# A fused banded attention and two-layer block on one core: the planner of all engines' orders gets other durations, a model of transfers, and a pass back and forth

## The chip, the cores and the metric

The kernel runs on one core of a Trainium2 chip. The metric is the device time of one execution in microseconds (us). Three runs of the kernel before took 677.65, 678.53 and 680.7 us, a median of 678.53 us.

## The reference

Attention over 4 batches, 8 heads, 768 positions, 64 wide, keeps for each query the first 4 keys (sinks) and the last 128 keys. Its output, 3072 tokens of 512, goes through two matrix products with a gate between them.

```python
scores = scale * np.matmul(q, k.transpose(0, 1, 3, 2))
keep = is_sink | in_window              # key < 4, or 0 <= query - key < 128
a = softmax(np.where(keep, scores, -1e9))
x = np.matmul(a, v)                     # then (3072, 512)
h = x @ w_in                            # (512, 2048)
g = h - np.tanh(h)
return g @ w_out                        # (2048, 512)
```

## The kernel before

**Tiles.** The 3072 tokens are 12 chunks of 256. A chunk's attention is four units, one for each pair of heads. The 2048 hidden columns are 8 groups of 256. One step is one chunk with one group; 96 steps, listed in `order`, are the two-layer block. Each step has a first half (24 matmuls at L807 into a double-buffered PSUM tile `h`), a gate, and a second half (L877, or from chunk 5 on L911, which computes 2x2 blocks of the product with seven products instead of eight). All products are split into a high and a low part. In the seven-product form the gate is a chain: tanh on ACT (L826), a difference (L829) and three sums (L840 to L842) on DVE, a copy to the high part on ACT (L845), and the low part on DVE (L848). One buffer, `gbuf`, is held from its tanh to its low part.

**A unit of attention** loads keys and queries (L347, and L356 or L104), computes scores on PE (L517 for the first 12 units, L524 later), masks and reduces them on DVE (`merge`: L539 and L541), takes exp and scales on ACT (L549, L575), turns them on PE (L609), masks them (L616 to L629), and multiplies by the values on PE (L666, L672). The result becomes `xall` on ACT and DVE (L688, L692).

**Weights** arrive as 64-bit words (`wraw`, L402), are decoded on DVE (L156 to L160) and split. The first matrix is written back to memory (`wscr`) and, from chunk 3 on, streamed through a ring of seven slots (`ring` and `spare`, L792); four slots make one step's weights. Sums of blocks of the second matrix are made by a copy and an accumulating transfer (`derive`, L1006 and L1009).

**Queues.** SP issues the loads of the first 12 units, weights, ring and most stores; GpSimd (POOL) issues keys, queries and values of later units, the accumulating transfers and most stores of the result. An engine executes in the order in which its instructions were emitted, so one that waits holds all behind it on that engine.

**The order is planned.** Nothing is emitted while the program is described: each piece of work is put into `Work` with its engine, a duration, a due time, and the names it reads and writes. `Work.order` then simulates all engines. At each moment it takes, of the pieces that are ready, the one with the smallest due time. The pieces are emitted by their simulated start, and that is each engine's order on the chip; the simulated times themselves do not reach the chip. Due times come from formulas with constants (`due_step`, `due_unit`, `due_group`). In the planner before, a transfer keeps SP occupied for `lands` ns and its data is there 1700 ns later, or 4372 ns (`LAND`) later for pieces due after 65222 (`LATE`); from then on the durations of ACT, DVE and POOL are also multiplied by 1.05. Pieces marked `port` wait while one marked so runs on the other of DVE and POOL.

The lines that the steps below speak of:

```python
n = min((n for n in waiting[e] if at(n, e) <= t), key=lambda n: (self.all[n][2], n))   # due time decides
...
todo, _ = work.order()
for n in todo:
    work.all[n][3]()                    # emitted in the order of simulated starts
```

Of the kernel before, what the change touches and what calls it, by code (L numbers as in the profile page):

```python
# [32 lines left out]
NG = 8  # L33
# [135 lines left out]
class Work:  # L169
# [3 lines left out]


    WAKE = {"PE": 250, "ACT": 170, "DVE": 90, "POOL": 100, "SP": 80}

    def __init__(self, slack, pad, late, land):
        self.all, self.wrote, self.read = [], {}, {}
        self.slack, self.pad, self.late, self.land = slack, pad, late, land

    def add(self, engine, took, due, fn, reads=(), writes=(), lands=0, port=False):
# [10 lines left out]
        self.all.append((engine, took, due, fn, after - {n}, lands, port))  # L192

    def order(self):
        todo = {}
        for n, (engine, *_) in enumerate(self.all):
            todo.setdefault(engine, []).append(n)
        users, left = [[] for _ in self.all], [len(t[4]) for t in self.all]
# [3 lines left out]
        ready = {n: 0.0 for n, k in enumerate(left) if k == 0}  # L202
        waiting = {e: [n for n in v if n in ready] for e, v in todo.items()}
        free, port, start, done = dict.fromkeys(todo, 0.0), {}, {}, {}

        def at(n, e):
            t = max(free[e], ready[n])
            return max(t, port.get("DVE" if e == "POOL" else "POOL", 0.0)) if self.all[n][6] else t

        while any(waiting.values()):  # L210
            t, e = min((min(at(n, e) for n in v), e) for e, v in waiting.items() if v)
            n = min((n for n in waiting[e] if at(n, e) <= t), key=lambda n: (self.all[n][2], n))
            _, took, _, _, _, lands, locks = self.all[n]
            took *= self.pad if e in ("ACT", "DVE", "POOL") and self.all[n][2] > self.late else 1.0
            waiting[e].remove(n)
            start[n], free[e], done[n] = t, t + took, t + took
            if lands:
                free[e], done[n] = t + (took if e == "POOL" else lands), t + lands + (1700 if self.all[n][2] < self.late else self.land)
            if locks:
                port[e] = t + took  # L220
            for u in users[n]:
                f = self.all[u][0]
                lag = 0 if f == e else self.WAKE[e]
                if f == "PE":
                    lag += self.slack if self.all[u][2] > self.late else 100
                ready[u] = max(ready.get(u, 0.0), done[n] + lag)
                left[u] -= 1
                if not left[u]:
                    waiting[f].append(u)
# [3 lines left out]
def _banded(tc, qd, kp, vp, vs, masks, w_in, w_out, ident, pts, early, out):  # L233
    nc = tc.nc
    et = mybir.EngineType
    with ExitStack() as ctx:
# [27 lines left out]
        RAW, TWO, CUT, DUO, SC, PB, ZL, TK = 12, 12, 2, 3, 4, 4, -4000, 1100  # L264
        SLK, PAD, LATE, LAND, QP, KP, BP, LEAD3 = 0.0, 1.05, 65222.0, 4372.0, 0, 0, 1, 89032.0
        SA, NSLOT, RING, GP, LQ, ST = 5, 7, 7, 0, 1, 1
        work = Work(SLK, PAD, LATE, LAND)
# [61 lines left out]
        def load_qk(u):  # L329
# [36 lines left out]
            if raw(u):  # L366
                work.add("POOL", 460, t - ZL, zeros, (), [slots(u)[1]])
# [6 lines left out]
        def load_v(cc):  # L374
# [19 lines left out]
            work.add("POOL" if LQ and cc > 3 else "SP", 500 * took, due_unit(4 * cc), values, (), [vslot[cc, i] for i in new] + ["seq v"],  # L394
                     lands=1000 * took)

        def load_w(k, g):
# [10 lines left out]
            for z in range(2):  # L408
                work.add("SP", 500, t, lambda z=z: words(z), (), [("wr", k, g, z)] + old, lands=2050)
# [28 lines left out]
        work.add("POOL", 900, 1500, sink_start, (), ["sidei", "vsink"] + [("z", i) for i in range(NPAIR)])  # L438
        work.add("ACT", 600, 0, rest, (), ["mask"])
        count = [0]  # L440

        def sink_values(b, due):
# [23 lines left out]
            work.add("SP", 400, due - 9000, load, (), [slot], lands=300)  # L466
            work.add("ACT", 500, due - 3500, high, [slot], ["vsink"])
            work.add("POOL", 1000, due - 3000, low, ["half", "vsink"], [slot], port=True)
            work.add("DVE", 500, due - 1000, total, [slot], ["vsink"], port=True)
# [4 lines left out]
        def split(u):  # L474
# [26 lines left out]
            work.add("ACT", 525, t, q_high, q, ["qh"] + old)  # L501
            work.add("POOL" if QP else "DVE", 1360 if QP else 705, t, q_low, q + ["qh"], ["ql"], port=True)
            for h in range(2):
                work.add("ACT", 425, t, lambda h=h: k_high(h), k, [("ks", h)] + old)
                work.add("POOL" if KP else "DVE", 1050 if KP else 590, t, lambda h=h: k_low(h), k, [("ks", h)], port=True)

        def scores(u, t):
# [48 lines left out]
            if raw(u):  # L556
                src, took = slots(u), 890
# [805 lines left out]
```

## Time and profile before

| | us |
|---|---|
| median of three runs | 678.53 (677.65 to 680.7) |
| span of the profiled execution, first to last instruction | 676.2 |
| PE busy | 655.5 (97%) |
| PE weight loads busy | 603.3 (89%) |
| DVE busy | 531.8 (79%) |
| ACT busy | 412.6 (61%) |
| POOL busy | 204.0 (30%) |

The page gives the profiled execution by its span; a whole-execution time of that same run is not listed, and the median of the runs is 2.3 us above the span. Transfers took 153 MB, 226 GB/s over the span: 57.4% of the 16 DMA engines' time went to the queue that SP fills (q1), 16.4% to the one that POOL fills (q0). The mean granted TensorE clock was 0.997 of full speed. The page's slices show PE at 60% in the first fortieth, 80% in the second, at 90% or more in 37 more, and at 50% in the last.

### The profile page before, as it was taken

The page shows a single profiled execution, that of the slowest core. Times are in us where ns is not written, and L with a number is a line of the kernel's source. Part 1 is how long each engine was busy: PE and PEld are TensorE (multiplying, and loading weights), DVE is VectorE, ACT ScalarE, POOL GpSimd, SP SyncE. Part 2 cuts the span into 40 slices and gives each one's busy share as a digit, 9 for nine tenths or more (in the row PEclk, how much of TensorE's full clock was granted, in tenths as well). Part 3 has the DMA queues.
Part 4 walks back from the last instruction along what each step waited for, and adds up shares of the span by engine and source line. Part 5 has one row for each costly group of instructions (what it writes and reads, how often), then busy time and mean ns, then how long its engine had stood idle before and what let it go on. Part 6 is the DMA issues. An engine that isn't in the chain of part 4 may idle for free.

```text
span 676.2 us, 14570 instructions
## 1 busy us (share of the span) xinstructions
PE 655.5 (97%) x5099; PEld 603.3 (89%) x5099; DVE 531.8 (79%) x1365; ACT 412.6 (61%) x1056; POOL 204.0 (30%) x363
## 2 busy tenths in 40 slices
PE   6899999999999999999999999999999999999995
PEld 4677899998988899889999999999999999999995
DVE  6889998964898975567798898888988878855654
ACT  4986443435998876556776667567667567632331
POOL 5454000001995443344523323332223322300100
PEclk9999999999999999999999999999999999999998
DMA  5878797786998677799977767867777766657861
GB/s 177 266 262 269 266 295 263 270 287 175 191 203 274 203 217 223 227 280 266 300 217 240 224 199 207 260 196 203 227 231 216 242 199 199 198 165 207 270 198 37
DMA packets 79341, 152.96 MB, mean 226 GB/s; under 512 B 9564, under 2 KB 25564, under 8 KB 79260
## 3 DMA queue, kind: packets, MB, share of 16 engines
q1 hardware_dynamic: 65884, 121.65, 57.4%
q0 software_dynamic: 13376, 30.30, 16.4%
q8 instruction: 42, 0.69, 0.4%
q14 instruction: 39, 0.32, 0.1%
HBM read 131.47 MB, written 20.45 MB: 225 GB/s over the span
## 4 chain that ended last, share of the span: by engine, by line
PE 73%; ACT 7%; DVE 5%; DMA 5%; POOL 4%; issue 4%; POOLq 0%; SPq 0%; DVEq 0%; ACTq 0%
PE h L807 30%; PE s L911 10%; PE o L911 7%; PE o L877 6%; PE x L672 3%; PE s L877 3%; DMA w<-bscr 2%; PE t L609 2%; PE t L672 2%; PE t L877 2%; PE t L524 2%; PE x L877 2%; ACT p L575 2%; PE x L524 1%; ACT p L549 1%
## 5 line engine op out<-in xcount | busy, mean ns | idle before, releaser
L807 PE MATMUL h<-xall,ring 128*128 128x256 f32 x990 | 130.9, 279 | 0.0
L807 PEld LDWEIGHTS h<-xall,ring 128*128 128x128 f32 x990 | 121.2, 188 | 0.9 <-PE t L672 0.2
L826 ACT ACTIVATE gbuf<-h 128x512 f32<-128x512 f32 x96 | 57.1, 595 | 84.6 <-PE h L807 55.2
L356 POOL DMA_DIRECT2D qraw<-qd x36 | 29.3, 813 | 222.4 <-DVE q L496 198.0
L807 PE MATMUL h<-xall,spare 128*128 128x256 f32 x738 | 96.2, 277 | 0.0
L807 PEld LDWEIGHTS h<-xall,spare 128*128 128x128 f32 x738 | 90.0, 188 | 0.5
L549 ACT ACTIVATE p<-p,st 128x132 f32<-128x132 f32 x168 | 66.9, 400 | 26.8 <-DVE st L541 25.5
L845 ACT CAST ghbuf<-gbuf 128x896 fp32r<-128x896 f32 x55 | 51.9, 943 | 49.3 <-DVE gbuf L842 48.8
L848 DVE TENSOR_TENSOR glbuf<-gbuf,ghbuf 128x896 fp32r<-128x896 f32 x55 | 60.3, 1096 | 19.7 <-ACT ghbuf L845 16.0
L575 ACT ACTIVATE p<-p,st 128x132 f32<-128x132 f32 x168 | 54.2, 394 | 3.9 <-DVE st L570 3.5
L829 DVE TENSOR_TENSOR gbuf<-h,gbuf 128x512 f32<-128x512 f32 x55 | 37.8, 687 | 19.1 <-ACT gbuf L826 18.7
L877 PE MATMUL o<-w,ghbuf 128*128 128x512 f32 x192 | 50.8, 399 | 0.3
L629 POOL TENSOR_TENSOR pt<-pt,after 128x512 f32<-128x512 f32 x32 | 44.4, 1386 | 22.0 <-ACT pt L626 21.3
L807 PE MATMUL h<-xall,w 128*128 128x256 f32 x384 | 50.5, 282 | 0.0
L807 PEld LDWEIGHTS h<-xall,w 128*128 128x128 f32 x384 | 48.5, 188 | 1.6
L829 DVE TENSOR_TENSOR h<-h,gbuf 128x512 f32<-128x512 f32 x41 | 28.5, 694 | 19.1 <-ACT gbuf L826 19.0
L488 DVE TENSOR_TENSOR ks<-kraw,ks 64x392 fp32r<-64x392 f32 x72 | 40.4, 562 | 3.4 <-ACT ks L483 1.1
L877 PEld LDWEIGHTS o<-w,ghbuf 128*128 128x128 f32 x192 | 33.8, 188 | 6.8 <-ACT ghbuf L832 0.9
L623 DVE TENSOR_TENSOR pt<-t,below 128x512 f32<-128x512 f32 (+1 forms) x48 | 28.8, 600 | 12.6 <-PE t L609 7.4
L483 ACT CAST ks<-kraw 64x392 fp32r<-64x392 f32 x72 | 37.1, 515 | 2.2 <-DMA kraw<-kp 1.4
L911 PE MATMUL s<-edge,ghbuf 128*128 128x256 f32 x220 | 35.5, 280 | 0.1
L835 DVE TENSOR_TENSOR glbuf<-h,ghbuf 128x512 fp32r<-128x512 f32 x41 | 28.1, 685 | 9.1 <-ACT ghbuf L832 9.1
(174 smaller groups left out, 1560.8 us busy)
## 6 DMA issues: line engine op xcount, KB each, us to landing
ring<-wscr SPq DMA_DIRECT2D x165, 256.0 KB, 4.3
spare<-wscr SPq DMA_DIRECT2D x123, 256.0 KB, 4.6
qraw<-qd POOLq DMA_DIRECT2D x36, 256.0 KB, 5.0
wraw<-w_in SPq DMA_DIRECT2D x16, 512.0 KB, 6.0
wraw<-w_out SPq DMA_DIRECT2D x16, 512.0 KB, 5.7
wscr<-w SPq DMA_DIRECT2D x16, 512.0 KB, 6.0
kraw<-kp POOLq DMA_DIRECT2D x36, 196.0 KB, 4.6
v<-vp POOLq DMA_DIRECT2D x18, 256.0 KB, 3.4
```

Source lines behind the costliest of these rows:

```text
L483: nc.scalar.copy(ks[u][r, h, :], kt[u][r, :])
L488: (nc.gpsimd if KP else nc.vector).tensor_tensor(k[o, h, :], t[r, :], k[r, h, :].bitcast(F32), op=ALU.subtract)
L549: nc.scalar.activation(e, e, AF.Exp, bias=st[u][:, j : j + 1], scale=-1.0, accum_out=st[u][:, 4 + j : 5 + j],)
L575: nc.scalar.activation(pr[u][:, j, :], pr[u][:, j, :], AF.Copy, scale=s[:, 8 + j : 9 + j])
L629: nc.gpsimd.tensor_tensor(w[:, :, 0, :], w[:, :, 0, :], after.unsqueeze(1).to_broadcast([P, 4, P]), op=ALU.mult)
L807: nc.tensor.matmul(hps[n][:, f, :], lhsT=w, rhs=x, start=r == 0, stop=r == 11)
L826: nc.scalar.activation(g0, h(), AF.Tanh)
L829: nc.vector.tensor_tensor(g0 if strassen(n) else h(), h(), g0, op=ALU.subtract)
L845: nc.scalar.copy(ghbuf[:, n % 2], gbuf[:, 1:, :])
L848: nc.vector.tensor_tensor(glbuf[:, :7, :], gbuf[:, 1:, :], ghbuf[:, n % 2].bitcast(F32), op=ALU.subtract)
L877: nc.tensor.matmul(sums_of(n, cc, t), lhsT=a[:, f, t * P : (t + 1) * P], rhs=wt[1, g][:, (0, 1, 0)[i], f, :], start=first and not low and ...
L911: nc.tensor.matmul(acc, lhsT=a[:, b, :], rhs=factor(g, m, part % 2), start=g == 0 and part == 0 and m in (4, 1, 2, 7), stop=closes(n) and ...
```

## The change

`Work` is replaced and the figures handed to it are changed; what is computed, the tiles, and the due-time formulas stay.

1. Durations and wake-up times between engines are other numbers (DVE pieces of 705 become about 605; a masked `merge` goes from 880 to 1091; a first-half piece on PE from 722 to 685). The 1.05 factor and the constants `SLK`, `PAD`, `LATE`, `LAND`, `TK` go. Every result that goes from another engine to PE counts as 400 ns later (`SLACK`).
2. All transfers share one "mover": each carries `moves`, the time it takes there, and has landed `LOAD` = 2700 (or `STORE` = 1400) after its turn. SP is occupied only for the issue and issues at most 1000 ns (`AHEAD`) before the mover is free.
3. `order` first packs with the due times, then packs backward from the end with the reversed order as rank, then forward again with the backward pass's start times as rank (`TURNS` = 1). That last pass gives the order.
4. The tokens "seq k" and "seq q", which kept the loads of keys and those of queries in order among themselves, go; "seq v" stays.
5. `x_high` makes its tiles at its first call in whatever order, where it did so in the call for the first pair.

```diff
-    WAKE = {"PE": 250, "ACT": 170, "DVE": 90, "POOL": 100, "SP": 80}
+    WAKE = {"PE": 200, "ACT": 150, "DVE": 118, "POOL": 75, "SP": 80}
+    AHEAD, SLACK = 1000, 400
...
+    def lag(self, a, u):
+        e, lands = self.all[a][0], self.all[a][5]
+        return (lands or (0 if e == self.all[u][0] else self.WAKE[e])) + self.SLACK * (e != "PE" and self.all[u][0] == "PE")
+
+    def pack(self, rank, back=False):
+
+        users = [[] for _ in self.all]
         for n, t in enumerate(self.all):
             for a in t[4]:
                 users[a].append(n)
+        then = [t[4] for t in self.all] if back else users
+        left = [len(u) if back else len(t[4]) for u, t in zip(users, self.all)]
+        ready, waiting, free, start = {}, {t[0]: [] for t in self.all}, {}, {}
...
         def at(n, e):
+            t, moves = ready[n], self.all[n][7]
+            if back and moves:
+                t = max(t, free.get("mover", 0.0)) + moves
+            elif moves and e == "SP":
+                t = max(t, free.get("mover", 0.0) - self.AHEAD)
+            t = max(t, free.get(e, 0.0))
+            return max(t, free.get("port of DVE" if e == "POOL" else "port of POOL", 0.0)) if self.all[n][6] else t
 
         while any(waiting.values()):
             t, e = min((min(at(n, e) for n in v), e) for e, v in waiting.items() if v)
-            n = min((n for n in waiting[e] if at(n, e) <= t), key=lambda n: (self.all[n][2], n))
-            _, took, _, _, _, lands, locks = self.all[n]
-            took *= self.pad if e in ("ACT", "DVE", "POOL") and self.all[n][2] > self.late else 1.0
+            n = min((n for n in waiting[e] if at(n, e) <= t), key=lambda n: (rank[n], -n if back else n))
             waiting[e].remove(n)
-            start[n], free[e], done[n] = t, t + took, t + took
-            if lands:
-                free[e], done[n] = t + (took if e == "POOL" else lands), t + lands + (1700 if self.all[n][2] < self.late else self.land)
...
+            _, took, _, _, _, _, port, moves = self.all[n]
+            start[n] = t
+            free[e] = done = t + took
+            if port:
+                free["port of " + e] = done
+            if moves:
+                free["mover"] = t if back else max(done, free.get("mover", 0.0)) + moves
+                done = done if back else free["mover"]
+            for u in then[n]:
+                lag = self.lag(u, n) if back else self.lag(n, u)
+                ready[u] = max(ready.get(u, 0.0), done + lag)
                 left[u] -= 1
                 if not left[u]:
-                    waiting[f].append(u)
+                    waiting[self.all[u][0]].append(u)
+        return start
+
+    def order(self):
+        start = self.pack([t[2] for t in self.all])
+        for _ in range(self.turns):
+            last = self.pack({n: -s - self.all[n][1] for n, s in start.items()}, back=True)
+            start = self.pack({n: -s - self.all[n][1] for n, s in last.items()})
         return sorted(start, key=lambda n: (start[n], n)), start
...
-            work.add(e, 600, t, keys, (), [slots(u)[0], "seq k"], lands=800 if raw(u) else 1000)
-            work.add(e, 800, t, queries, (), [slots(u)[1], "seq q"], lands=600 if raw(u) else 1000)
+            work.add(e, 430 if raw(u) else 564, t, keys, (), [slots(u)[0]], lands=LOAD, moves=630)
+            work.add(e, 1120 if raw(u) else 745, t, queries, (), [slots(u)[1]], lands=LOAD, moves=424 if raw(u) else 848)
...
-            work.add("DVE", 880 if kind else 450, d + 1000, merge, s + ["mask"] * (0 < kind), [("p", slot(u), i) for i in range(t, 2)])
+            work.add("DVE", 1091 if kind else 434, d + 1000, merge, s + ["mask"] * (0 < kind), [("p", slot(u), i) for i in range(t, 2)])
...
-            work.add("SP", 400, d, copied, src, w + old, lands=took + 100)
-            work.add("POOL", 650, d, added, src, w, lands=1000 + 600 * n)
+            work.add("SP", 430, d, copied, src, w + old, lands=LOAD, moves=424 * n)
+            work.add("POOL", 585, d, added, src, w, lands=LOAD, moves=809 * n)
...
-                    work.add("SP", 500, due_step(n) - STREAM + 700 * j, lambda j=j: stream(n, j),
-                             [("scr", g, j // 2)], [("ring", ring_at(n, j))] + ([("w", 0, 1)] if cc == 3 and g == 0 else []), lands=850)
+                    work.add("SP", 320, due_step(n) - STREAM + 700 * j, lambda j=j: stream(n, j),
+                             [("scr", g, j // 2)], [("ring", ring_at(n, j))] + ([("w", 0, 1)] if cc == 3 and g == 0 else []), lands=LOAD, moves=810)
...
-                    work.add("PE", 722, due_step(n) - LAST * (n == NS - 1), some, x + [w], [("h", n % 2)])
+                    work.add("PE", 685, due_step(n) - LAST * (n == NS - 1), some, x + [w], [("h", n % 2)])
```

## Rows read from the trace of the kernel before

**Rows 1.** The page's first part: busy us, share of the span and instructions by engine.
```profile
PE 655.5 (97%) x5099; PEld 603.3 (89%) x5099; DVE 531.8 (79%) x1365; ACT 412.6 (61%) x1056; POOL 204.0 (30%) x363
```
**Rows 2.** Busy time by stretch; its first line names the columns.
```profile
core 0: us, PE busy (x) PEld busy (x) DVE busy (x) ACT busy (x) POOL busy (x), PEclk, DMA share, GB/s
0.00:20.00 20.00, 13.05 (x53) 9.38 (x54) 12.58 (x71) 11.16 (x42) 10.37 (x36) 1.00 0.59 182
20.00:75.00 55.00, 51.12 (x342) 40.10 (x341) 50.50 (x158) 42.97 (x146) 21.75 (x44) 1.00 0.80 264
...
150.00:225.00 75.00, 73.38 (x503) 64.53 (x502) 60.73 (x181) 60.53 (x175) 46.77 (x70) 1.00 0.85 218
...
350.00:600.00 250.00, 248.94 (x2201) 240.87 (x2200) 213.41 (x571) 163.26 (x406) 73.05 (x128) 1.00 0.70 214
...
650.00:676.20 26.20, 19.21 (x155) 17.98 (x153) 13.04 (x24) 5.81 (x8) 0.00 (x0) 0.92 0.31 94
```
**Rows 3.** PE's waits over the span: total us, times, longest.
```profile
PE s L517 <- DMA qk<-qd: 3.3, 2, 1.7
...
PE t L609 <- ACT pt L616: 1.9, 3, 1.0
```
**Rows 4.** SP's timeline from 6.5 to 17 us: start, duration, line, transfer.
```profile
8.39 1.05 SPq L391 DMA_DIRECT2D v<-vp  x2
9.49 0.43 SPq L347 DMA_DIRECT2D qk<-kp  x1
...
11.17 0.67 SPq L446 DMA_DIRECT2D vraw<-vs  x1
11.89 0.43 SPq L402 DMA_DIRECT2D wraw<-w_in  x1
12.36 0.43 SPq L347 DMA_DIRECT2D qk<-kp  x1
```
**Rows 5.** DVE's waits from 12 to 20 us.
```profile
DVE st L569 <- ACT wide L549: 1.2, 1, 1.2
DVE wide L541 <- PE s L517: 1.1, 1, 1.1
```
**Rows 6.** DVE's timeline: one masked merge, its first instruction and the next piece's.
```profile
17.93 0.27 DVE L539 COPY_PREDICATED o<-above,o 128x128 f32<-128x128 uint32 x1
...
19.01 0.73 DVE L461 SCALAR_TENSOR_TENSOR vsink<-vsink,sides,vraw 64x128 fp32r<-64x128 f32 x2
```
**Rows 7.** SP's timeline from 57 to 75 us.
```profile
58.11 6.33 SPq L391 DMA_DIRECT2D v<-vp  x3
64.49 0.90 SPq L402 DMA_DIRECT2D wraw<-w_in  x2
```
**Rows 8.** The timeline near the end: one gate's first and last instruction.
```profile
658.71 0.60 ACT L826 ACTIVATE gbuf<-h 128x512 f32<-128x512 f32 x1 [1.68 <-PE h L807]
...
662.17 1.09 DVE L848 TENSOR_TENSOR glbuf<-gbuf,ghbuf 128x896 fp32r<-128x896 f32 x1 [1.01 <-ACT ghbuf L845]
```
**Rows 9.** Busy time by stretch of L848 alone, one for each step.
```profile
350.00:600.00 250.00, 41.76 (x38) 1.00 0.70 214
```
**Rows 10.** Transfers from 175 to 225 us: queue share, then ring loads' median landing.
```profile
q0 software_dynamic: 4047, 6.06, 58.0%
...
ring<-wscr SPq DMA_DIRECT2D x8, 256.0 KB, 6.7
```
**Rows 11.** The same two rows from 325 to 600 us.
```profile
q0 software_dynamic: 4959, 14.82, 16.5%
...
ring<-wscr SPq DMA_DIRECT2D x96, 256.0 KB, 3.8
```
**Rows 12.** The timeline's end: last low part, PE's last pieces, DVE's last sums.
```profile
668.03 0.68 DVE L835 TENSOR_TENSOR glbuf<-h,ghbuf 128x512 fp32r<-128x512 f32 x1
668.77 0.73 PE L877 MATMUL t<-w,glbuf 128*128 128x512 f32 x2 [0.75 <-DVE glbuf L835]
...
669.53 0.69 DVE L985 TENSOR_TENSOR wide<-t,wide 128x512 f32<-128x512 f32 x1 [0.82 <-PE t L877]
```

More of the change, by code (lines that the diff above doesn't have):

```diff
@@ L169, with __init__, add @@
 class Work:
-    WAKE = {"PE": 250, "ACT": 170, "DVE": 90, "POOL": 100, "SP": 80}
[L177 to L181, printed above, removed]
+    WAKE = {"PE": 200, "ACT": 150, "DVE": 118, "POOL": 75, "SP": 80}
+    AHEAD, SLACK = 1000, 400
+    def __init__(self, turns):
+        self.all, self.wrote, self.read, self.turns = [], {}, {}, turns
+    def add(self, engine, took, due, fn, reads=(), writes=(), lands=0, moves=0, port=False):
         n = len(self.all)
@@ L191, in add @@
             self.wrote[w], self.read[w] = n, []
[L192 to L198, printed above, removed]
+        self.all.append((engine, took, due, fn, after - {n}, lands, port, moves))
+    def lag(self, a, u):
[3 more added lines that the diff above has]
+        users = [[] for _ in self.all]
         for n, t in enumerate(self.all):
@@ new lines, in pack @@
+        ready, waiting, free, start = {}, {t[0]: [] for t in self.all}, {}, {}
+        for n, k in enumerate(left):
+            if not k:
+                ready[n] = 0.0
+                waiting[self.all[n][0]].append(n)
+        def at(n, e):
+            t, moves = ready[n], self.all[n][7]
[5 more added lines that the diff above has]
+            return max(t, free.get("port of DVE" if e == "POOL" else "port of POOL", 0.0)) if self.all[n][6] else t
@@ L393, in load_v @@
             took = len(new)
-            work.add("POOL" if LQ and cc > 3 else "SP", 500 * took, due_unit(4 * cc), values, (), [vslot[cc, i] for i in new] + ["seq v"],
-                     lands=1000 * took)
+            pooled = LQ and cc > 3
+            work.add("POOL" if pooled else "SP", (553 if pooled else 530) * took, due_unit(4 * cc), values, (), [vslot[cc, i] for i in new] + ["seq v"],
+                     lands=LOAD, moves=810 * took)
         def load_w(k, g):
@@ L436, in sink_half @@
             nc.vector.tensor_copy(sides, sidei)
-        work.add("POOL", 900, 1500, sink_start, (), ["sidei", "vsink"] + [("z", i) for i in range(NPAIR)])
-        work.add("ACT", 600, 0, rest, (), ["mask"])
+        work.add("POOL", 712, 1500, sink_start, (), ["sidei", "vsink"] + [("z", i) for i in range(NPAIR)])
+        work.add("ACT", 295, 0, rest, (), ["mask"])
         count = [0]
@@ L464, in total @@
                     )
[L466 to L469, printed above, removed]
+            work.add("SP", 591, due - 9000, load, (), [slot], lands=LOAD, moves=231)
+            work.add("ACT", 520, due - 3500, high, [slot], ["vsink"])
+            work.add("POOL", 1447, due - 3000, low, ["half", "vsink"], [slot], port=True)
+            work.add("DVE", 642, due - 1000, total, [slot], ["vsink"], port=True)
         qh, ql, ks, pr, st, xps, xh, xl, sps, tps = ({} for _ in range(10))
@@ L631, in turn @@
             d = due_unit(u) + 5500
[L632 removed]
+            work.add("PE", 440, d, transposes, [("p", slot(u), 0), ("p", slot(u), 1)], ["t"])
             if c == 0:
[L634 to L635 removed]
+                work.add("ACT", 252, d + 1400, whole, ["t"], [("pt whole", m)])
+            work.add("DVE", 334 if c == 0 else 608, d + 1500, lambda: part(1, below), ["t"], [("pt own", m)])
             if c and BP:
[L637 to L638 removed]
+                work.add("ACT", 482, d + 1500, plain, ["t"], [("pt before", m)])
+                work.add("POOL", 1293, d + 1600, masked, (), [("pt before", m)], port=True)
             else:
[L640 removed]
+                work.add("DVE", 334 if c == 0 else 608, d + 1500, lambda: part(0, after), ["t"], [("pt before", m)])
         def attend(cc, p0, pairs):
@@ L678, in x_high @@
             def x_high(i):
-                if p0 == 0 and i == 0:
+                if cc not in xh:
                     if home(cc) == 2:
@@ L988, in end @@
                 for t in range(2):
[L989 to L990 removed]
+                    work.add("DVE", 609, d + 10000, lambda t=t: add4(t), ["tx"[t]], [("end", t)] + o)
+                    work.add("SP", 338, d + 11000, lambda t=t: put(t), [("end", t)], (), lands=STORE, moves=810)
             ends_with.append(end)
@@ L1079, in second_half @@
                 r = [(("gh", "gl")[low], n % 2), ("w", 1, g)]
-                work.add("PE", 464 if low else 928, due_step(n) + HALF2, some, r, [bank(cc, t)])
+                work.add("PE", 467 if low else 934, due_step(n) + HALF2, some, r, [bank(cc, t)])
             if n == NS - 1:
```

122 lines of the change are left out of this document (50 added, 72 removed).

## The prediction

> **What bounds the kernel now.** I read the page's engine shares first, then busy time by stretch, then PE's waits, and last the timelines of the places where PE waits. The shares say that PE is busy for 655.5 of 676.2 us [rows 1]. The change removes no matmul, so a better order can at most take away the other 20.7 us. The stretches say where these lie [rows 2]. From 0 to 20 us PE lacks 6.95 us, from 20 to 75 us 3.88 us, from 150 to 225 us 1.62 us, from 350 to 600 us only 1.06 us, and from 650 us on 6.99 us. These five make 20.5 us; the reader should see that the four hundred microseconds in which most of the work is done have almost nothing to give. Part of the two ends is no order's to change: warm-up and first loads, and the last sums and stores. DVE is the second engine: 50.50 of 55 us from 20 to 75 us, and 213.41 of 250 us from 350 to 600 us [rows 2]. In the first of these stretches it limits how early PE can get weights and attention results; in the second it has 15% free. So the change is a reordering of a kernel that is bound by PE's work, with possible gains at the start and possible losses anywhere.
>
> **The change part by part.**
>
> *Issue and landing of the first loads.* PE waits twice for queries in the first 20 us, 3.3 us together [rows 3]. On SP, the two transfers of values (1.05 us) go ahead of a unit's keys, and a sink load and a first piece of weights go between that unit and the next: from 11.17 us to the next keys at 12.36 us is 1.19 us [rows 4]. Keys and queries of each unit issued alone would start 1.10 us earlier (9.49 less 8.39) for the first, and 1.10 plus 1.19, 2.3 us, for the second. The values are read only after scores, exp and the turn, so by the start times of a backward pass they rank behind both units' loads; by the due times they did not. DVE can follow: it idles 1.2 and 1.1 us there [rows 5]. The gain lies between 2.3 us and a loss of 1.2 us (a weight piece or value load put ahead of one more unit costs what the pair in rows 4 costs); I take 2.0 us, because nothing else that PE needs in this time is on SP.
>
> *Durations on DVE between 20 and 75 us.* The planner before counts a masked merge as 880 ns; on the chip one takes 19.01 less 17.93, 1.08 us [rows 6]. One stands in each of the first twelve units, so the plan runs 0.2 us further ahead of the chip with each, and PE is sent to pieces whose input isn't there: after the queries its largest wait is for the copy of turned blocks on ACT, whose bank the next turn needs, 1.9 us in three waits [rows 3]. New figures (1091, and 334 instead of 430 for such a block) put that right. In the same stretch one values load holds SP for 6.33 us, and the next weights are issued only at 64.49 us, right behind it [rows 7]; a plan that knows when the buffer comes free issues the weights first. Both together can give at most PE's missing 3.88 us [rows 2], and nothing if DVE's 50.50 of 55 us is the limit whatever the order. A loss is possible too: one decode piece put ahead of a unit's merge; two such of about the length of that merge would be 2.2 us. I take half of the missing time, 1.9 us.
>
> *The 400 ns before PE, and the wake-up times.* No instruction is added; a piece on PE is only moved behind others until its input is 400 ns old. That costs nothing while PE has other work, which is the first halves of the next step; where there is none, PE would wait anyway. PE lacks 1.62 us from 150 to 225 us and 1.06 us from 350 to 600 us [rows 2], 2.7 us together. I take half, 1.4 us; the ends are all of it, and a loss that I price with the rivals.
>
> *Loads counted later or earlier.* A ring load was planned as landing 850 + 4372 = 5.2 us after its issue. Now it is 320 + 810 + 2700 = 3.8 us behind a free mover, and 0.4 us more ahead of PE. From 325 to 600 us the chip shows a median of 3.8 us [rows 11], from 175 to 225 us 6.7 us [rows 10]. In the long stretch this is right and changes nothing, since the slot's release, not the landing, decides when the load goes out. In the crowded one it is a rival below; in the sum it stands at zero, between a gain of the 1.62 us missing there (already counted) and the rival's loss.
> The Trainium skill, page "DMA: Bandwidth & Descriptors", section "Queues, rings and completion order", says that each DMA engine takes packets from its queues in turn. By that rule, one mover that serves whole transfers in order is the wrong picture whenever SP and POOL both have transfers out, because a ring load then shares the engines to its end. The trace agrees: 6.7 us where POOL's queue took 58.0% [rows 10], 3.8 us where it took 16.5% [rows 11]. By the rule alone the time would be that of the transfer rival, 683.5 us.
>
> *Tokens dropped.* Keys and queries of different units may now pass each other on SP, and on POOL behind the scale and mask pieces. Later units share one buffer each for keys and queries, which keeps them in order anyway; for the first twelve it is part of the first term. Alone it is worth 0, with the first term's ends.
>
> *The end.* The last low part on DVE starts at 668.03 us, behind sums that nothing needs until 669.53 us, and PE waits 0.75 us for it [rows 12]. Ranked by the latest start it goes ahead of them. PE ends 0.75 us sooner, but the displaced sums then stand just before the last ones; I take 0.6 us, between 0 and 0.75.
>
> *Waits.* No semaphore wait is added for its own sake. But a new order changes what stands behind a waiting instruction: on SP a transfer that waits for its buffer holds ring loads, as the 6.33 us did for weights [rows 7], and PE is who waits for these. On POOL it holds the sinks and masks of the unit at work.
>
> Sum: 2.0 + 1.9 + 1.4 + 0.6 = 5.9 us. The span goes from 676.2 to 670.3 us. What lies around it I take as it stands, 2.3 us (678.5 less 676.2, from two different executions), so 672.6 us, some 0.9% faster. The ends of the same terms, without the rivals, are 2.3 + 3.9 + 2.7 + 0.75 = 9.6 us of gain, and 1.2 + 2.2 = 3.4 us of loss. As the likeliest case's own range I give 668.9 to 675.1 us.
>
> **The rivals.**
>
> *The transfers come late (slower).* Place: 175 to 225 us, the most crowded stretch. The plan believes 3.8 us, the chip shows 6.7 us [rows 10], so PE would be sent to a first half whose weights are 2.9 us away. Part is covered: with seven slots and four to a step, a slot's next load has six quarters of a first half, 6 x 0.685 = 4.1 us, plus a second half in some steps. What is left is 6.7 less 4.1, 2.6 us, where no second half stands between, and nothing where one does. There are eight of these loads [rows 10]; at 1.1 us each, less than half of the 2.6, that is 9 us, less the 4 us from the start that would stay: 678.5 + 9 - 4 = 683.5 us. It decides from the point where the load is issued less than 6.7 us before its use. For it: the longest landings in rows 10. Against it: the slots' release already paces these loads, and PE lost only 1.62 us there with the order before.
>
> *The gate's chain gets interrupted (slower).* From its tanh at 658.71 to the end of its low part at 663.26 us a gate takes 4.55 us [rows 8], and one buffer serves all gates, so a step can't be shorter. From 350 to 600 us there are 38 steps in 250 us [rows 9], 6.58 us each. DVE is busy 213.41 / 38 = 5.62 us per step; some 2.9 us are the gate's, 2.7 us the next attention's. If the latter never falls into the gaps that ACT's two pieces leave (some 1.5 us), a step takes 4.55 + 2.7 = 7.25 us, 0.67 us too long: 25 us in 38 steps. It decides when more than 2.0 us of other work stand inside the chain. Ranks by latest start put gates and attention close to one another, where the due formulas held them apart by whole steps; that is for it. That DVE still has 15% free, and that two `h` tiles let PE go ahead, is against it. At half the price it would be 678.5 + 12.5 - 4 = 687 us.
>
> *Nothing in sum (same).* DVE holds PE from 20 to 75 us whatever the order, and what the first loads give is lost in the middle: 675.5 to 681.5, about 678 us. For it: 50.50 of 55 us [rows 2], and less than 2 us of PE's time missing in most long stretches.
>
> *All of it.* The terms' upper ends, and with them waits that PE's pipelining hides within its busy time: 665 us. For it: the plan's durations now fit the chip; against it: the ends of the run are mostly start-up and the last chain.
>
> *That it doesn't do what it says.* If the ranks of the last pass came out as the old order, the time would be 678.5 us; it is in the case of no change.
>
> **How the numbers follow.** Forecast 0.43, all of it 0.11, same 0.21, transfers late 0.12, chain interrupted 0.13. A measurement of this kernel tells some 0.5%, 3.4 us, from no change. Faster than 675.1 us is the forecast and the larger gain, 0.54; slower than 681.9 us the two slow rivals, 0.25; the rest 0.21. The range goes from 664 us, below the larger gain, to 687 us, the middle of the chain's price; about 0.06 lies beyond the upper end and 0.05 below the lower one, and the cases of both signs between make it this wide.
>
> **What would show it.** In the changed kernel's trace: the wait of PE for queries gone or under 1.5 us, and keys and queries issued ahead of values; PE's busy time from 20 to 75 us above 52.5 us; PE's busy time from 350 to 600 us still above 248 us, or else the chain; no wait of PE for ring loads from 175 to 325 us, or else the transfers; the last low part ahead of the sums. The prediction is wrong if PE lacks more than 8 us between 75 and 650 us, or if DVE's order at the start moves PE's first step of the block later than before.

## The result and the profile after

The changed kernel takes 684.55 us, the median of 6 runs (682.84 to 686.48), against 678.32 us for the kernel before beside it: a ratio of 1.0083 with the interval [1.0062, 1.0105]. The forecast was 672.6 us. The time is inside the range, the direction is wrong. The profiled execution's span is 684.1 us, 7.9 us longer than [rows 1, 2].

The page's shares, beside [rows 1]:

```profile
PE 658.7 (96%) x5099; PEld 604.7 (88%) x5099; DVE 537.9 (79%) x1365; ACT 412.5 (60%) x1056; POOL 202.1 (30%) x363
```

The instruction counts are the same to the last one. PE is busy 3.2 us longer and lacks 25.4 us instead of 20.7; the two make the 7.9 us. DVE is busy 6.1 us longer with the same instructions, which an order alone should not do.

Busy time by stretch, beside [rows 2], with two short windows at the end:

```profile
0.00:20.00 20.00, 14.16 (x56) 10.79 (x56) 13.29 (x75) 12.57 (x49) 11.97 (x39) 1.00 0.60 182
20.00:75.00 55.00, 51.65 (x343) 40.19 (x344) 49.47 (x152) 42.23 (x139) 15.70 (x39) 1.00 0.89 305
...
150.00:225.00 75.00, 71.31 (x479) 62.15 (x478) 61.12 (x184) 59.46 (x175) 46.74 (x70) 0.98 0.75 191
225.00:300.00 75.00, 74.47 (x541) 65.59 (x540) 52.94 (x156) 52.73 (x148) 29.59 (x53) 1.00 0.71 219
300.00:350.00 50.00, 48.48 (x368) 43.79 (x367) 29.12 (x71) 26.91 (x63) 16.67 (x24) 1.00 0.94 259
350.00:600.00 250.00, 245.86 (x2165) 239.17 (x2164) 215.92 (x555) 158.91 (x390) 72.46 (x128) 1.00 0.69 219
600.00:650.00 50.00, 49.84 (x448) 48.33 (x447) 32.69 (x70) 19.73 (x36) 4.72 (x8) 1.00 0.63 196
...
210.00:215.00 5.00, 3.54 (x26) 3.13 (x26) 4.67 (x17) 4.95 (x16) 2.54 (x6) 1.00 1.01 306
215.00:220.00 5.00, 3.69 (x11) 3.11 (x12) 4.45 (x16) 3.71 (x13) 1.96 (x5) 0.66 0.89 319
```

Two stretches of the kernel before, for the same comparison:

```profile
225.00:300.00 75.00, 75.00 (x555) 67.25 (x554) 51.73 (x149) 50.64 (x139) 28.64 (x49) 1.00 0.76 225
300.00:350.00 50.00, 49.81 (x390) 45.70 (x390) 36.70 (x93) 32.66 (x81) 20.73 (x33) 1.00 0.95 274
```

PE gained 1.11 us in the first stretch and 0.53 in the second. Then it lost 2.07 us from 150 to 225 us and 3.08 us from 350 to 600 us; from 225 to 350 us, where the kernel before lacked 0.19 us, it lacks 2.05. Between 75 and 650 us PE now lacks 10.0 us (0.16 of them after 600), where it lacked 2.9. The loss is in the middle. PE's longest waits over the whole span, without the one before its first instruction:

```profile
PE t L540 <- DVE pt L639: 3.1, 3, 1.8
PE o L893 <- ACT ghbuf L848: 2.5, 2, 2.4
PE x L666 <- POOL z L602: 2.4, 4, 1.3
PE s L533 <- DVE st L585: 1.9, 2, 1.7
PE s L533 <- DVE st L557: 1.9, 2, 1.5
```

The two rows of L533 are waits of the first 40 us. The others stand almost wholly in the middle, and four of them make most of its loss: 2.38 us at 216 us for a gate, 1.26 us at 314 us for the sinks' weights from POOL (L602), and 1.76 and 0.95 us at 356 and 586 us for the mask of turned blocks on DVE (L639). No wait for a transfer is among them, and the queries' 3.3 us of [rows 3] are gone. The longest wait, read in the timeline, with the end of the run behind it:

```profile
208.12 1.31 POOL L645 TENSOR_TENSOR pt<-pt,after 128x512 f32<-128x512 f32 x1
208.27 1.20 DVE L585 TENSOR_SCALAR st<-st 128x4 f32<-128x4 f32 x1
...
211.75 0.58 ACT L842 ACTIVATE gbuf<-h 128x512 f32<-128x512 f32 x1
214.38 0.69 DVE L845 TENSOR_TENSOR h<-h,gbuf 128x512 f32<-128x512 f32 x1
215.70 0.56 ACT L848 CAST ghbuf<-h 128x512 fp32r<-128x512 f32 x1
216.31 1.97 PE L893 MATMUL o<-w,ghbuf 128*128 128x512 f32 x4 [2.38 <-ACT ghbuf L848]
...
674.83 1.09 PE L893 MATMUL t<-w,ghbuf 128*128 128x512 f32 x4
...
676.01 0.68 DVE L851 TENSOR_TENSOR glbuf<-h,ghbuf 128x512 fp32r<-128x512 f32 x1
676.61 0.74 DVE L979 TENSOR_TENSOR wide<-o,wide 128x256 f32<-128x256 f32 x2
```

A gate's tanh ends at 212.33 us, and its difference on DVE starts only at 214.38: DVE did attention in between, and ACT did attention and a sum of blocks of the second matrix before the high part at 215.70. PE stood for 2.38 us and paid twice: the granted clock from 215 to 220 us was 0.66 of full speed, so for some of that time it was at the lower of its two levels (1.2 instead of 2.4 GHz), and four 128x512 matmuls took 1.97 us there against 1.09 us later. Earlier, at 208.27 us, a DVE instruction on 128x4 numbers took 1.20 us; it started 0.15 us after POOL's mask and ended with it. The mean of each form shows that this isn't a single case. Before, after, and the kernel with a thin mask (told below); behind the bar stand the busy time in us and the mean in ns:

```profile
L629 POOL TENSOR_TENSOR pt<-pt,after 128x512 f32<-128x512 f32 x32 | 44.4, 1386 | 22.0 <-ACT pt L626 21.3 <-DMA qraw<-qd 0.3
...
L496 DVE TENSOR_TENSOR q<-qraw,q 128x512 fp32r<-128x512 f32 x36 | 25.8, 715 | 4.6 <-ACT q L493 4.6
L840 DVE TENSOR_TENSOR gbuf<-gbuf 128x256 f32<-128x256 f32 x55 | 23.3, 424 | 1.6
L842 DVE TENSOR_TENSOR gbuf<-gbuf 128x128 f32<-128x128 f32 x55 | 16.1, 292 | 1.9
```
```profile
L645 POOL TENSOR_TENSOR pt<-pt,after 128x512 f32<-128x512 f32 x32 | 45.0, 1406 | 27.3 <-ACT pt L642 27.3
...
L512 DVE TENSOR_TENSOR q<-qraw,q 128x512 fp32r<-128x512 f32 x36 | 29.1, 808 | 1.3 <-ACT q L509 1.0
L856 DVE TENSOR_TENSOR gbuf<-gbuf 128x256 f32<-128x256 f32 x55 | 26.0, 474 | 1.7
L858 DVE TENSOR_TENSOR gbuf<-gbuf 128x128 f32<-128x128 f32 x55 | 18.5, 337 | 1.9
```
```profile
L645 POOL TENSOR_TENSOR pt<-pt,after 128x16 f32<-128x16 f32 x32 | 10.3, 320 | 29.8 <-ACT pt L642 29.8
...
L512 DVE TENSOR_TENSOR q<-qraw,q 128x512 fp32r<-128x512 f32 x36 | 24.7, 686 | 1.4 <-ACT q L509 1.1
L856 DVE TENSOR_TENSOR gbuf<-gbuf 128x256 f32<-128x256 f32 x55 | 23.3, 425 | 1.7
L858 DVE TENSOR_TENSOR gbuf<-gbuf 128x128 f32<-128x128 f32 x55 | 16.1, 293 | 1.9
```

Taking every DVE instruction that is over 120 ns longer than the median of its form, and adding what is above the median, gives 4.1 us in 9 instructions before, 13.3 us in 17 after, 0.4 us in 2 with the thin mask. DVE and POOL get in each other's way more often in the new order.

### The profile page after: what moved, and what is told of

Read it like the earlier page. It is cut to its first block, busy times and chain, and to the rows that moved or that the text cites. A ratio compares the mean times of both kernels' runs of the same rounds, so it can differ in the third digit from the quotient of the medians.

```text
span 684.1 us, 14568 instructions
## 1 busy us (share of the span) xinstructions
PE 658.7 (96%) x5099; PEld 604.7 (88%) x5099; DVE 537.9 (79%) x1365; ACT 412.5 (60%) x1056; POOL 202.1 (30%) x363
## 4 chain that ended last, share of the span: by engine, by line
PE 61%; DVE 16%; ACT 8%; DMA 6%; issue 5%; POOL 2%; SPq 0%; DVEq 0%; POOLq 0%; ACTq 0%
PE h L823 26%; PE s L927 7%; PE o L893 6%; PE o L927 5%; DMA w<-bscr 4%; PE s L893 3%; PE x L688 3%; PE t L893 2%; PE x L893 2%; PE t L688 2%; DVE ks L504 1%; DVE gbuf L845 1%; DVE pt L639 1%; DVE p L557 1%; PE t L625 1%
## 5 line engine op out<-in xcount | busy, mean ns | idle before, releaser
L823 PE MATMUL h<-xall,ring 128*128 128x256 f32 x990 | 127.1, 277 | 0.0
L823 PEld LDWEIGHTS h<-xall,ring 128*128 128x128 f32 x990 | 119.7, 188 | 0.7
L645 POOL TENSOR_TENSOR pt<-pt,after 128x512 f32<-128x512 f32 x32 | 45.0, 1406 | 27.3 <-ACT pt L642 27.3
L927 PE MATMUL o<-w,ghbuf 128*128 128x256 f32 x220 | 35.2, 279 | 0.0
L927 PE MATMUL s<-w,ghbuf 128*128 128x256 f32 x220 | 34.9, 277 | 0.0
```

Of the source, the lines that this page charges most:

```text
L645: nc.gpsimd.tensor_tensor(w[:, :, 0, :], w[:, :, 0, :], after.unsqueeze(1).to_broadcast([P, 4, P]), op=ALU.mult)
L823: nc.tensor.matmul(hps[n][:, f, :], lhsT=w, rhs=x, start=r == 0, stop=r == 11)
L927: nc.tensor.matmul(acc, lhsT=a[:, b, :], rhs=factor(g, m, part % 2), start=g == 0 and part == 0 and m in (4, 1, 2, 7), stop=closes(n) and ...
```

## The experiments

Each time is a median, with its ratio to the kernel before on the same chip (679.3 to 680.2 us). "Figures" are the durations, wake-up times and landings; "passes" are the backward and the forward packing. The expectations name their theories by letters: A the plan has no reserve, B the passes' ranks, C the derived blocks' transfers, D the durations, M the mover and its landings, P the port that DVE and POOL share, S scatter, V that the old figures are good for a reason.

**The passes or the figures?** First the new figures without passes, then the old figures with them.

```diff
-SA, NSLOT, RING, GP, LQ, ST, TURNS, LOAD, STORE = 5, 7, 7, 0, 1, 1, 1, 2700, 1400
+SA, NSLOT, RING, GP, LQ, ST, TURNS, LOAD, STORE = 5, 7, 7, 0, 1, 1, 0, 2700, 1400
```


> The changed kernel with TURNS = 0: new durations, wake-ups, slack and mover, but the order of the due times, without the passes back and forth. Theory A (the new figures hold no reserve, so each delay on the chip reaches PE): as slow as the changed kernel, 1.006 to 1.012 of before. Theory B (ranks by latest start put pieces just in time, the figures are harmless): 0.998 to 1.002. Theory C (the accumulating transfers of derive land later than planned and hold ACT and DVE): 1.006 to 1.010, since they are planned the same.

692.20 us, 1.0181 [1.0136, 1.0227]: slower than every band, so none of the three theories holds as stated.

```diff
 # the planner and all figures of before, and in order():
+        for _ in range(TURNS):
+            last = self.pack({n: -s - self.span(n) for n, s in start.items()}, back=True)
+            start = self.pack({n: -s - self.span(n) for n, s in last.items()})
```


> The kernel before with its own durations, landings and padding, and only the passes back and forth added to its planner. Theory A: 0.995 to 1.002 of before, the reserve is still there. Theory B: 1.006 to 1.012, like the changed kernel. Theory C: 0.996 to 1.002, transfers are planned as before.

676.60 us, 0.9960 [0.9939, 0.9980]. So the passes help with either set of figures (some 7.7 us with the new, 2.8 with the old), and B is refuted. With passes in both, the new figures cost 684.55 - 676.60 = 8.0 us; the two were timed on different chips, and their ratios say 1.2%, which is 8.4 us.

**Transfers of derived blocks, and a plain reserve.** In the plan of the changed kernel the copies of `derive` land 1500 ns and its accumulating transfers 2500 ns later; then, in another kernel, all pieces of ACT, DVE and POOL are 5% longer.

```diff
-            work.add("SP", 430, d, copied, src, w + old, lands=LOAD, moves=424 * n)
-            work.add("POOL", 585, d, added, src, w, lands=LOAD, moves=809 * n)
+            work.add("SP", 430, d, copied, src, w + old, lands=LOAD + 1500, moves=424 * n)
+            work.add("POOL", 585, d, added, src, w, lands=LOAD + 2500, moves=809 * n)
```


> The changed kernel with one thing other: derive's copies are planned to land 1500 ns later and its accumulating transfers 2500 ns later. Theory A: 1.003 to 1.008, only this part of the reserve comes back. Theory B: 1.006 to 1.010. Theory C: 0.997 to 1.003, and ACT's waits for w<-bscr fall from 9.4 us to under 4 us.

700.14 us, 1.0307 [1.0273, 1.0340]. ACT's wait for these blocks in the changed kernel, and in this one:

```profile
ACT w L1028 <- DMA w<-bscr: 9.4, 5, 4.7
```
```profile
ACT w L1028 <- DMA w<-bscr: 0.9, 2, 0.5
```

The wait went from 9.4 to 0.9 us and the kernel got slower, in an order planned anew: taking this wait away does not bring the time back. C, which had 0.997 to 1.003, is refuted as stated; A and B missed too.

```diff
+            took *= 1.05 if e in ("ACT", "DVE", "POOL") else 1.0
```


> The changed kernel with the durations of ACT, DVE and POOL multiplied by 1.05 in all passes. Theory A: 0.995 to 1.002 of before. Theory B: 1.005 to 1.010. Theory C: 1.005 to 1.010.

690.37 us, 1.0180 [1.0141, 1.0219]. A reserve of this form makes it worse; A as stated fell.

**One half of the figures at a time,** both with passes: new durations, wake-up times and 400 ns with the old landings; then the new mover and landings with the old durations. The dropped tokens belong to the second half.

> The planner of e2 (transfers as before, passes back and forth) with the new durations, wake-ups and the 400 ns of the change, without the 1.05. Theory D (the durations, cut to the chip's best, take the reserve out of the plan): 1.006 to 1.018 of before. Theory M (the mover and the short landings do the harm): 0.994 to 1.000, like e2.

684.87 us, 1.0064 [1.0043, 1.0084].

> The changed kernel's planner, mover, landings and passes, with the durations, wake-ups and 1.05 of before and no 400 ns. Theory D: 0.992 to 1.000 of before. Theory M: 1.006 to 1.018.

684.46 us, 1.0063 [1.0036, 1.0090]. D's band holds in the first of the two runs and M's in the second: beside 676.60 us each half alone costs as much as both together, so neither D nor M is the whole answer.

**The port.** The mask on POOL is cut to 4 of 128 columns, in the changed kernel and in the one before. Both leave the rest of the masking undone; the order is that of the full kernel.

```diff
-nc.gpsimd.tensor_tensor(w[:, :, 0, :], w[:, :, 0, :], after.unsqueeze(1).to_broadcast([P, 4, P]), op=ALU.mult)
+nc.gpsimd.tensor_tensor(w[:, :, 0, :4], w[:, :, 0, :4], after[:, :4].unsqueeze(1).to_broadcast([P, 4, 4]), op=ALU.mult)
```


> The changed kernel, every engine's order as it is, but POOL's mask of the block before (L645) works on 4 of 128 columns only, so that POOL leaves the memory port to DVE. Left out: the mask of the other columns. Theory P (DVE is held by POOL's masks, and the new plan puts more of DVE's gate pieces beside them): DVE's busy time falls by 6 us or more, and the time to 0.992 to 0.999 of before. If the port isn't the cause: 1.004 to 1.008, as only POOL's own late sinks gain.

677.55 us, 0.9949 [0.9928, 0.9969].

> The kernel before with the same thin mask (L629), order unchanged. Theory P: little to gain, 0.994 to 0.999 of before, so that e7 and e8 come within 0.4% of each other. If the port isn't the cause: e8 as e7's gain, and the two still 0.8% apart.

678.89 us, 0.9977 [0.9949, 1.0005]. Both times lie in P's bands. The thin mask takes 7 us off the changed kernel and nothing sure off the one before. That looked like the whole answer, but the run takes away two things: the collision, and 1.1 us of the way from turned block to product (320 instead of 1406 ns per mask). The next runs keep the work whole. They let DVE mask straight out of PSUM, in place of ACT's copy and POOL's mask, and plan anew.

```diff
-QP, KP, BP, LEAD3 = 0, 0, 1, 89032.0
+QP, KP, BP, LEAD3 = 0, 0, 0, 89032.0
```


> The changed kernel with the one switch BP from 1 to 0, so that all 32 masks of the cross-chunk part of the attention weights are made by DVE straight out of PSUM, where ACT copied (32 pieces by 482 ns in the plan) and POOL masked (32 by 1293). Nothing is left out of the computation. The order is planned anew from it (plan's end 650.2 us against 649.4). DVE gets 32 x 688 ns = 22.0 us of work that reads one input in SBUF and one in PSUM, and loses the stretch beside the mask. Theory P (the loss is DVE instructions held up while POOL's mask runs): DVE busy about 525.4 + 22.0 = 547 us, hardly an instruction of DVE over 120 ns longer than its kind's median (after: 17 us in 24), and a time like that of the thin mask, 677.5, plus what a fuller DVE costs: 676 to 681 us, ratio to before 0.995 to 1.002. Theories D and M (the new durations, the new mover: the order is tighter than the chip follows, whatever does the mask): the loss stays, 683 to 688 us, ratio 1.006 or more. Theory A (no reserve on DVE): a fuller DVE makes it worse than the changed kernel, above 686.

681.31 us, 1.0027 [1.0007, 1.0046]: just above P's band and below that of D and M, so neither holds as stated.

> The planner's figures of before, ordered by one backward and one forward pass (that was 676.6 us), and BP at 0: masks on DVE. Theory P: in that order POOL's mask cost little (3.7 us of stretched DVE instructions), and the thin mask took only 0.2% off the kernel before, so there is up to 2 us to win, less what 22.0 us more on DVE cost: 674 to 678 us, ratio 0.992 to 0.998. Rivals D and M say nothing against that: the figures are the old ones. Theory A (DVE as the next bound): above 680.

671.55 us, 0.9877 [0.9851, 0.9904]: faster than both kernels and than P's band, the best of all. In both, DVE's stretched instructions are down to 0.6 us in 3. Busy time by stretch, first the new figures, then the old:

```profile
20.00:75.00 55.00, 51.46 (x343) 40.00 (x342) 49.32 (x151) 41.99 (x138) 15.32 (x38) 1.00 0.92 309
...
150.00:225.00 75.00, 72.02 (x488) 61.97 (x487) 61.81 (x195) 58.12 (x173) 38.86 (x67) 1.00 0.78 199
225.00:300.00 75.00, 73.43 (x536) 64.92 (x535) 55.01 (x161) 48.54 (x137) 19.99 (x45) 1.00 0.69 216
```
```profile
20.00:75.00 55.00, 51.83 (x346) 40.88 (x346) 50.44 (x152) 43.39 (x143) 16.18 (x41) 1.00 0.80 266
...
150.00:225.00 75.00, 75.00 (x525) 67.63 (x524) 61.12 (x186) 57.91 (x168) 36.81 (x62) 1.00 0.86 222
225.00:300.00 75.00, 74.97 (x553) 66.81 (x552) 54.54 (x157) 47.22 (x134) 22.98 (x47) 1.00 0.77 225
```

With the collisions gone, PE lacks nothing from 150 to 225 us in the old figures' order and still 2.98 us in the new one's. So the collisions are real, and moving the masks is worth 684.55 - 681.31 = 3.2 us with the new figures and 676.60 - 671.55 = 5.1 with the old. How much of this the collisions are is open: the order is new, ACT's copy and POOL's mask are gone from a block's way, and in the old figures' order only 3.7 us had been stretched. But the collisions are not what tells the two apart: the new figures cost 681.31 - 671.55 = 9.8 us without them. P explains a cost that both kernels have.

Letting the plan hold the port longer does not do it either:

```diff
-                free["port of " + e] = done
+                free["port of " + e] = done + 400
```


> The changed kernel, where the plan holds the port that DVE and POOL share 400 ns past the end of each piece that takes it (plan's end 655.5 us against 649.4): the mask stays on POOL, whole. Nothing on the chip makes one engine keep the planned side of the other's piece, but the gap of 400 ns would let the order hold although the chip drifts from the plan. Theory P: fewer stretched instructions of DVE (under 8 us of excess against 13.3), and 677 to 682 us, ratio 0.996 to 1.003. If drift on the chip is larger than 400 ns, the excess stays above 10 us and the time at 683 to 688. Theories D and M: 684 or more, whatever the excess.

692.06 us, 1.0185 [1.0156, 1.0214], and DVE's excess stayed at 13.3 us, in 15 instructions. P's band is missed; the excess is that of the case with more drift than 400 ns, but the time is above its 683 to 688 us and fits only D and M.

**The halves again, with the masks on DVE,** and PE's pieces at their old sum.

> Before's transfers (SP's own landing times, no mover), the new durations of all pieces, the new wake times, the 400 ns and the passes, with the masks on DVE. It stands beside the order of old figures (671.55) and that of all new figures (681.31), both with the masks on DVE too. Theory D (the durations are what costs): 679 to 683 us, ratio 1.000 to 1.005. Theory M (the mover): 670 to 674, ratio 0.987 to 0.992. If each half costs by itself, as it did with the mask on POOL (684.87 and 684.46 beside 676.6): 676 to 682 in both.

684.43 us, 1.0074 [1.0051, 1.0098].

> The other half: the new mover and landings, with the old durations, old wake times, the factor 1.05 and no 400 ns, with the passes and the masks on DVE. Theory D: 670 to 674 us, ratio 0.987 to 0.992. Theory M: 679 to 683 us, ratio 1.000 to 1.005. Each half by itself: 676 to 682.

679.06 us, 1.0001 [0.9979, 1.0024]. Beside 671.55, the durations alone cost 12.9 us and the mover alone 7.5; both together 9.8. D missed both bands. M missed the first and met the second at its lower end (679 to 683 us), and "each by itself" missed the first and met the second.

```diff
+        took *= 1.04 if engine == "PE" else 1.0     # changed kernel, masks on DVE
```


> The changed kernel with the masks on DVE, and in the plan each of PE's pieces 4% longer, so that their sum is 662.6 us as in the old figures (662.4) and not 637.1; DVE, ACT, POOL and the mover as in the change. If the new plan is too tight because PE's pieces are taken as back to back, and so no reserve stands in the plan for the other engines beside PE: 672 to 676 us, ratio 0.989 to 0.996. If the relation of PE to the others isn't it: 679 to 684, as without (681.31).

700.83 us, 1.0324 [1.0299, 1.0350]: the guess was wrong by its sign, and its other case (679 to 684 us) missed too. Its waits of PE are again a gate's, and now also a ring load's:

```profile
PE o L894 <- ACT ghbuf L849: 3.9, 3, 2.4
...
PE h L824 <- DMA spare<-wscr: 2.0, 1, 2.0
```

**Is any other order slower, or is it these figures?** Small steps around both sets, masks on DVE: the factor 1.05 at 1.07, wake-up times 30 ns longer, PE's pieces 1% shorter; and 30 ns longer around the new figures.

> Old figures with the passes and the masks on DVE (671.55 us), the one number 1.05, by which the plan lengthens the pieces of ACT, DVE and POOL, set to 1.07. Theory S (scatter: any small change of a figure gives another order, whose time is a new draw; the old figures are one good draw): 675 to 690 us. Theory V (the old values are good for a reason, and so are their neighbours): 670 to 674.

675.00 us, 0.9934 [0.9912, 0.9957].

> The same order of old figures with 30 ns added to each wake time (PE 280, ACT 200, DVE 120, POOL 130, SP 110). Theory S: 675 to 690 us. Theory V: 670 to 674.

674.85 us, 0.9925 [0.9898, 0.9952].

> The same order of old figures with PE's pieces 1% shorter in the plan (sum 655.8 us against 662.4). Theory S: 675 to 690 us. Theory V: 670 to 674.

674.00 us, 0.9913 [0.9880, 0.9945].

> The changed kernel with the masks on DVE (681.31 us) and 30 ns added to each wake time. The plan's own end moves from 650.2 to 664.0 us by it. Theory S: a new draw, anywhere from 675 to 700 us. Theory V (the new values are bad for a reason, and so are their neighbours): 679 to 684.

694.64 us, 1.0216 [1.0176, 1.0255]. Neither theory holds as stated. Around the old figures the three times lie at the border of both bands, two just outside V's and one at its upper end; around the new ones V's band is missed by 10 us and S's holds. A small step moves the time by some 3 us around the old figures, where all four orders beat the kernel before, and by 13 us in the one step around the new ones. So 671.55 is a good draw of a place worth some 674 us, and differences of a few us between two single orders say little. What does not hang on one order: the ten kernels here that do the whole work with the new durations, or a small change of them, took 681.31 us or more, all slower than the kernel before; the five with the old figures and the passes took 676.60 or less, all faster.

The end of each plan (the issue of its last store), beside the chip's span, shows another difference. With the old durations and landings the chip keeps pace with the plan: before 676.0 planned and 676.2 measured, old figures with passes 674.9 and 673.9, with masks on DVE 673.8 and 672.3. With the old durations and the new mover it is some us behind: 674.4 and 682.1, with masks on DVE 673.3 and 678.5. With the new durations it falls far behind: 649.4 planned and 684.1 measured in the changed kernel, 655.6 and 683.5 with the old landings and masks on DVE, 664.0 and 693.2 with 30 ns more. Much of that is PE: its pieces sum to 637.1 us in the new plan, and it was busy for 658.7 us. But a plan that ends nearer to the chip's time is not a better order: with PE's pieces 4% longer the plan ends at 681.7 and the span is 697.3 us, only 15.6 us behind, in the slowest kernel of all. My reading, which no run tested by itself: pieces that the plan puts side by side meet on the chip shifted against each other, and PE's waits of 1 to 3 us come of that.

## Why the prediction was wrong

The forecast added up gains, 5.9 us, from an order that was taken to fit better because its figures do. The runs split the change otherwise: the passes by themselves gain some 2.8 us, and the new figures cost some 8.0 us on top of them (0.4% and 1.2%, which make the 0.8% measured). The prediction's own sign of being wrong, more than 8 us that PE lacks between 75 and 650 us, came: 10.0. That the time lies inside the range is luck, since its upper end of 687 us stood for the gates of all 38 steps interrupted at half price, which the trace doesn't show.

*The first loads (2.0 us).* Right in what happens: the first two units' keys and queries go ahead of the values, and the wait for queries is gone. Half of its worth was taken by the next wait, DVE, up to 1.7 us at L533, which I had dismissed because DVE idles there [rows 5]. PE has 1.1 us more in the first 20 us, where 2.0 were forecast.

*Durations on DVE, 20 to 75 us (1.9 us).* Worth 0.53 us; the 52.5 us that the prediction asked for was not reached (51.65). Even the best kernel has 51.83 us there, so DVE's 50 of 55 us seems close to the limit, as the rival "nothing in sum" had it.

*The 400 ns, the wake-up times and the middle (1.4 us).* This step failed, together with its premise, on which the rival "all of it" leant too: that figures which fit the chip piece by piece give an order which fits better. It priced the two middle stretches as a gain of half of the 2.7 us that PE lacked there, because moving a piece behind others was to cost nothing while PE has other work. PE lost 2.07 and 3.08 us in them instead, and 7.1 us between 75 and 650 us. With the passes and the masks on DVE the new durations, wake-up times and 400 ns cost 12.9 us by themselves (8.3 with the mask on POOL). I should have read the small number the other way: a stretch where PE lacks 1.06 of 250 us [rows 2] is one in which an order has next to nothing to win and much to lose. Four waits of 0.95 to 2.38 us, for a gate, for the sinks' weights and twice for a mask of turned blocks, make most of the loss.

*The end (0.6 us).* Right: the low part goes ahead of the last of those sums (L979), and PE's 0.75 us of [rows 12] are gone. From the last difference to the last sum on DVE it is 5.5 us, before 6.4.

*Loads and tokens (0).* This term, put at nothing, failed too, though not by the way that its rival named. Ring loads land in 5.1 us median from 175 to 225 us, where [rows 10] had 6.7, and PE never waits for one from 175 to 325 us: the rival of late transfers is refuted there, and its 683.5 us is near the result by accident. But the new mover and landings, with the tokens dropped, cost 7.9 us by themselves with the mask on POOL and 7.5 with it on DVE, through the order that they give. The Trainium skill's rule of page "DMA: Bandwidth & Descriptors", section "Queues, rings and completion order", may hold, but the loss that I drew from it isn't in the trace.

*The gate's chain.* Its place and its mechanism, attention between the gate's pieces, were nearest: the wait at 216 us is that. From 350 to 600 us PE's busy time fell to 245.86, under the 248 that it named, but there the waits are mostly of attention itself: scores (L540) wait until DVE has masked the turned blocks in their bank (L639), 3.1 us in three. Its 0.33 us for each of 38 steps was not seen. The prediction named no cost of POOL's mask beside DVE, though the `port` marks in the planner point to one; a rival "DVE and POOL collide where the plan's order drifts" was missing, and moving the masks gave 3 to 5 us.

What stays open is which of the new durations does it, and how. A uniform reserve on three engines, and one on PE, both made it slower. The 400 ns, the wake-up times and the dropped tokens were not tried by themselves.

## What to carry to other kernels

A planner's figures are part of a working order. Durations that fit each piece can leave out what stands between pieces, and where the chip ends 35 us behind the plan, pieces may no longer meet as they were planned; so compare the plan's end with the measured span before trusting a shorter plan. Try small steps around a set of figures before reading anything into one order. Change the algorithm and the figures separately: here the passes alone won 0.4% and, with the masks moved to DVE, 1.2%, while all together lost 0.8%. Where the bound engine lacks 1 us in 250, price a new order as a risk.

## What the runs showed of the hardware

A DVE instruction can be held up whole by POOL's mask: one of 128x4 took 1.20 us at 208.27 us, against a mean of 0.171 us with the thin mask, and ended with the mask. With the masks on DVE the stretched instructions went from 13.3 to 0.6 us. The Trainium skill, page "SBUF — State Buffer", section "Who interferes with whom", says of the port pair that DVE and GpSimd share that it is "an exclusive lock"; the trace agrees with its numbers here. Masking out of PSUM on DVE took 0.68 us each, 32 x 0.679 = 21.7 us more work on DVE, and the kernels with it, planned anew, were still faster.

A wait of PE of 2.38 us, up to 216.31 us, cost more than its length: the granted clock was 1.00 in the window of 5 us before 215 us and 0.66 in the one behind, and four matmuls right behind the wait took 1.97 us instead of the 1.09 us that four such took at 674.83 us, 0.88 us more.
